# Gated mix of two attentions on one core: one 64-row by 32-column tiling in the steps, relu banks from the scores' ring, output projection in pieces

## Chip, core and metric

The kernel runs on one core of a Trainium2 chip. The metric is the time of one execution on the device in microseconds (us); less is better. Before the change two runs took 2734.1 and 2738.14 us, median 2736.12.

## The reference, cut to what matters

Two attentions over the same input are mixed by a gate. S = 2048, D = 576, 32 heads of 18, all fp32.

```python
def _A_ref(x, wqkv, wo):                       # every head has keys and values of its own
    q, k, v = heads(x @ wqkv)
    p = softmax(einsum("bhqd,bhkd->bhqk", q, k) * 18 ** -0.5)
    return merge(einsum("bhqk,bhkd->bhqd", p, v)) @ wo
def _B_ref(x, wq, wk, wv, wo):                 # 32 query heads share one key and one value head
    ...
x = A_x
g = _sigmoid((x * gate_w).sum(-1, keepdims=True))
return g * a + (1 - g) * b
```

## The kernel before

The 64 heads (`NU`) are numbered u: the 32 of B first, then the 32 of A. A head's scores are 2048 by 2048 and are made transposed, keys on partitions: a *step* is one key tile i of 128 keys of one head, so there are 16 steps per head and `NSTEP` = 1024 in all, counted by T. The loop over T does two steps per pass, A (T) and B (T + 1); one pass is called a turn, eight turns make a head.

**Operands.** A query or key row is kept as high and low fp16 parts: 18 rows high, 18 high or low, 18 low or high, 54 partitions in all, and two more rows for the row maximum, 56 (`load_rows`, `max_rows`). Each operand lies twice in its tile: from partition 0 (`SB`) and from partition 64 (`MB`). A matmul on the first copy uses the upper half of the 128x128 array's rows, one on the second copy the lower half.

**Scores** (`step_scores`, matmul L446, exponential L453). Four matmuls per step, c = 0 to 3, each 128 keys by 512 queries, on the upper half, into a bank of the PSUM pool `ps_s` (3 banks); ScalarE takes the exponential out of the bank into an SBUF tile `pt` (ring of 12).

**Row maxima** (`step_max`, matmul L409) run `LEAD` = 22 steps ahead of the scores, since the scores' 55th and 56th rows subtract the maximum. They are made with queries on partitions: 128 queries by 512 keys on the lower half, into a bank of `ps_m` (4 banks), and VectorE reduces each bank to one column (L418). Of the eight chunks per turn one, A's chunk 1, is replaced by "x": keys of chunk 1 less keys of chunk 0 (`kd`) are multiplied, ScalarE takes the relu (L412) into SBUF, and VectorE adds it in one pass with chunk 0 of the same step (L415), so that VectorE has seven passes per turn and ScalarE nine. In the lead, T < 0, every chunk is reduced, and the maxima alternate with the projection of A's values (`project_v`, L252).

**PV** (`step_pv`, L459). The values with a column of ones, 19 columns, are the stationary operand; the four query chunks j go to four 32-column groups, 128 rows each, all into one bank `acc` that is kept over a head's 16 steps. The operands are fp32. The order strings cut a step's PV into column halves: `p` and `f` are the first and second 256 columns of the step two back, `h` and `H` of the step one back; `P` and `Q` do all 512 at once.

**End of a head** (`head_out`, L469). VectorE copies `acc` to SBUF, from where DMAs place the rows in a tile of 128 output features (`OT`) and the sums in DRAM. `normalise`, a generator advanced one yield per turn, divides the finished features by the sums, times the gate, and splits them on GpSimd into two f32r parts which go to DRAM (`on_d`).

**Output projection** (`out_proj`, matmul L575, evicted at L581 or L583). Three segments: feature tiles 0 to 3, 4 to 7 and 8. A unit is one output tile of 128 rows and 288 columns; it has three products of the split operands over the segment's tiles, 12 matmuls of 128x128 by 288, into a bank of `ps_m`. Segment 0 has its 32 units at fixed steps from T = 522 to 848 (`at_ends`, three in every two heads), segment 1 from 942 to 1008, about one per turn, segment 2 from 1021 on and behind the loop. What is left is the last head (`last_out`).

**Order.** All engines work through their queues in program order. Inside a turn that order is written out by hand as a string: `s` is a score chunk, `m` a maximum chunk, `x` the relu chunk, capitals A and B the step, then the letters of PV, `U` an output unit.

```python
PLAIN = "sA0 mA2 sA1 mA0 sA2 mA3 P sA3 mB0 sB0 mB1 sB1 mB2 h sB2 mB3 sB3 x H"
```

`END` and `AFTER` are used in the two turns around a head's end, `UNIT` where an output unit is due, `ALONE` when no maxima are left.

Of the kernel before, what the change touches and what calls it, by code (L numbers as in the profile page):

```python
# [8 lines left out]
F32 = mybir.dt.float32  # L9
# [5 lines left out]
OP = mybir.AluOpType  # L15
# [34 lines left out]
def gated_mix_kernel(ctx: ExitStack, tc: tile.TileContext, xT, wall, wv, wo, out):  # L50
# [10 lines left out]
    ps_m = ctx.enter_context(tc.tile_pool(name="ps_m", bufs=4, space=PSUM))  # L61
# [13 lines left out]
    on_d = [dram.tile([9 * P, S], F32, name=f"on{x}") for x in "hl"]  # L75
# [10 lines left out]
    acc = ps_o.tile([P, 512], F32, name="acc")  # L86

    nc.vector.memset(acc, 0.0)
# [308 lines left out]
    def step_max(u, i, c, low=False):  # L397
# [10 lines left out]
        pm = ps_m.tile([P, 512], F32, name="pm")  # L408
        nc.tensor.matmul(pm, qs[u % 3][b:b + 54, i * P:(i + 1) * P], k, start=True, stop=True)  # L409
# [30 lines left out]
    def step_scores(u, i, c, alone):  # L440
# [3 lines left out]
        if alone and c % 2:  # L444
            b = MB
        nc.tensor.matmul(ps, kst(u)[b:b + 56, i * P:(i + 1) * P],  # L446
                         qs[u % 3][b:b + 56, c * 512:(c + 1) * 512], start=True, stop=True)
# [8 lines left out]
    def step_pv(u, i, a, b):  # L456

        for j in range(4):
            nc.tensor.matmul(acc[32 * j:32 * j + 19, a:b], v_of(u, i), PT[u, i, j][:, a:b],  # L459
                             start=(i == 0 and a == 0), stop=(i == 15), skip_group_check=True)  # L460
        if b == 512:
            for j in range(4):
                del PT[u, i, j]
# [3 lines left out]
    def head_out(u):  # L467
        oe = L["work"].tile([P, 512], F32, name="oe", bufs=1)
        nc.vector.tensor_copy(oe, acc)  # L469
# [15 lines left out]
    def normalise(t, at_end=False):  # L485
# [32 lines left out]
        for c in range(4):  # L518
            cs = slice(512 * c, 512 * c + 512)
            h = L["work"].tile([P, 512], F32R, name="oh", bufs=1)  # L520
            l = L["work"].tile([P, 512], F32R, name="ol", bufs=1)
            nc.gpsimd.tensor_tensor(ot[:rows, cs], ot[:rows, cs], R[:rows, cs], op=OP.mult)
            yield
            split(ot[:rows, cs], h[:rows], l[:rows], nc.gpsimd, nc.gpsimd)
            yield
            yield
            dma(on_d[0][P * t:P * t + rows, cs], h[:rows])
            dma(on_d[1][P * t:P * t + rows, cs], l[:rows])
# [3 lines left out]

    def prep_wo(t0, rows):
        nt = len(rows)
        w = {y: L["pool"].tile([P, nt, D], F32R, name=f"wo{y}", tag=f"wo{y}{nt}") for y in "hl"}
# [9 lines left out]
    def out_proj(t0, rows, first=False):  # L545

        nt = len(rows)
        oacc = L["oacc"]
        O = {}

        def load(q):
            for x, y in enumerate("hl"):
                if "end" in L:
                    O[q, y] = L["end"][y][:, 256 * q:256 * q + 256].rearrange("p (t s) -> p t s", t=1)
                    continue
                t = L["pool"].tile([P, nt, 256], F32R, name=f"oi{y}", bufs=2)
                dma(t, on_d[x][P * t0:P * (t0 + nt), 256 * q:256 * q + 256]
                    .rearrange("(t p) s -> p t s", p=P))
                O[q, y] = t
# [3 lines left out]
        w = WO[t0]  # L563
        for q in range(8):
            if q < 7:
                load(q + 1)
            o = {y: O[q, y] for y in "hl"}
            for s2 in range(2):
                st_ = 2 * q + s2
                for hf in range(2):  # L570
                    fp = ps_m.tile([P, 512], F32, name="pm")
                    n = 0
                    for a, b in PRODS:
                        for t, r in enumerate(rows):
                            nc.tensor.matmul(fp[:, 0:288], o[b][:r, t, s2 * P:(s2 + 1) * P],  # L575
                                             w[a][:r, t, 288 * hf:288 * hf + 288],
                                             start=(n == 0), stop=(n == 3 * nt - 1))
                            n += 1
# [98 lines left out]
    def due(T, t0, t1, n):  # L677
        if t0 == SEG[0][3]:
            return at_ends.count(T)
# [96 lines left out]
```

## Time and profile before

| | |
|---|---|
| runs, median (lowest to highest) | 2736.12 us (2734.1 to 2738.14) |
| the profiled execution | 2735.79 us; span 2734.0 us |
| granted TensorE clock, mean | 0.991 |
| PE (matmuls), records | 2663.3 us busy, 97%, 22160 |
| VectorE (DVE) | 2430.7 us busy, 89% |
| ScalarE (ACT) | 2384.1 us busy, 87% |
| GpSimd (POOL) | 231.0 us busy, 8% |

PE is TensorE's matmuls and PEld its weight loads; a matmul's record reaches to its modelled end, so records of matmuls that follow each other overlap and a busy PE need not be one at its peak. A row of a timeline has start, length, engine, line, operation, operands and a count (merged records of one kind); a row by line has count, busy us, mean ns of one, and idle time before it with what ended it; a row by source has count, shortest, median and longest ns, and the first and last start. Releasers are inferred from semaphores. The main loop, T >= 0, starts 316 us into the span; the lead lies before it.

### The profile page before, as it was taken

What the parts mean: (1) busy time and instruction counts of PE and PEld (TensorE: products, weight loads), DVE (VectorE), ACT (ScalarE), POOL (GpSimd) and SP (SyncE); (2) the same over time, 40 slices, a digit from 0 to 9 for tenths busy, and PEclk for the clock granted to TensorE, in tenths of its full rate; (3) what the DMA queues carried; (4) which work ended last, traced back from release to release, by engine and by line L of the source; (5) the groups of instructions that cost most, each with busy time, mean ns of one, the idle gap of its engine ahead of it and who ended that gap; (6) DMA issues with size and microseconds to landing.
All of it is one profiled execution on the core that took longest, in us unless ns stands there. A gap on an engine that the chain in (4) does not pass through costs nothing.

```text
span 2734.0 us, 57725 instructions
## 1 busy us (share of the span) xinstructions
PE 2663.3 (97%) x22160; PEld 958.8 (35%) x22160; DVE 2430.7 (89%) x4582; ACT 2384.1 (87%) x4768; POOL 231.0 (8%) x438
## 2 busy tenths in 40 slices
PE   5899999999999999999999999999999999999999
PEld 3688522222222222222222333333333332223444
DVE  5345899999999999999999999999999999998875
ACT  3232499999999999999999999999999999998875
POOL 2221000001000200110110001000100020001000
PEclk9899999999999999999999999999999999999998
DMA  7232100001100100110132112112221122122312
GB/s 197 76 118 90 51 20 20 20 18 53 35 17 23 54 27 20 45 43 20 30 66 85 40 51 84 54 40 57 72 66 47 44 61 64 39 64 88 89 36 94
DMA packets 135321, 151.49 MB, mean 55 GB/s; under 512 B 55709, under 2 KB 104765, under 8 KB 133846
## 3 DMA queue, kind: packets, MB, share of 16 engines
q1 hardware_dynamic: 116156, 123.59, 16.2%
q10 hardware_dynamic: 14120, 13.65, 1.5%
q0 software_dynamic: 4768, 10.56, 1.2%
q8 instruction: 174, 2.85, 0.5%
q14 instruction: 103, 0.84, 0.1%
HBM read 92.02 MB, written 46.45 MB: 51 GB/s over the span
## 4 chain that ended last, share of the span: by engine, by line
ACT 54%; PE 37%; DVE 6%; DMA 2%; SPq 1%; issue 1%; DVEq 0%; ACTq 0%
ACT pt L453 48%; PE acc L459 12%; PE ps L446 11%; ACT xb L412 6%; PE ps L210 6%; PE pm L575 4%; DVE mx L418 3%; PE ps L252 2%; PE pm L409 2%; SPq L56 1%; DVE oe L469 1%; DVE junk L415 1%; DMA xs<-xT 0%; DVE oacc L629 0%; DVE oacc L583 0%
## 5 line engine op out<-in xcount | busy, mean ns | idle before, releaser
L453 ACT ACTIVATE pt<-ps 128x512 f32<-128x512 f32 x4052 | 2093.1, 637 | 68.4 <-PE pm L409 60.2
L418 DVE TENSOR_REDUCE mx<-pm 128x1 f32<-128x512 f32 x3096 | 1940.2, 682 | 89.5 <-PE pm L409 74.6
L446 PE MATMUL ps<-qs,ksb 56*128 56x512 f16 x2688 | 818.4, 380 | 10.8
L409 PE MATMUL pm<-ksb,qs 54*128 54x512 f16 x2364 | 738.5, 383 | 2.6 <-DVE mx L418 1.6
L459 PE MATMUL acc<-pt,vb 128*19 128x512 f32 (+1 forms) x6136 | 592.3, 458 | 1.9
L459 PE MATMUL acc<-pt,vg 128*19 128x256 f32 (+1 forms) x5664 | 579.5, 481 | 2.3 <-DVE oe L469 0.5
L409 PEld LDWEIGHTS <-qs 54*128 54x128 f16 x4096 | 330.0, 93 | 248.1 <-issue 195.2
L446 PE MATMUL ps<-qs,ksa 56*128 56x512 f16 x1364 | 404.4, 379 | 4.8 <-ACT pt L453 1.3
L446 PEld LDWEIGHTS <-ksb 56*128 56x128 f16 x2688 | 175.0, 94 | 622.5 <-issue 573.9
L409 PE MATMUL pm<-ksa,qs 54*128 54x512 f16 x1232 | 384.8, 382 | 0.6 <-ACT xb L412 0.4
L415 DVE CUSTOM_DVE_ANT_0 junk<-pm,xb 128x512 bf16<-128x512 f32 x500 | 339.9, 680 | 0.0
L412 ACT ACTIVATE xb<-pm 128x512 f32<-128x512 f32 x500 | 316.5, 633 | 0.0
L446 PEld LDWEIGHTS <-ksa 56*128 56x128 f16 x1408 | 89.3, 94 | 328.9 <-issue 299.0
L459 PEld LDWEIGHTS acc<-pt,vb 128*19 128x19 f32 x6136 | 104.1, 96 | 223.7 <-issue 206.6
L459 PEld LDWEIGHTS acc<-pt,vg 128*19 128x19 f32 x5664 | 96.0, 97 | 222.9 <-issue 204.9
L428 POOL TENSOR_SCALAR mt<-mt 128x32 f32<-128x32 f32 x64 | 18.6, 290 | 1616.4 <-DVE mt L426 1616.4
L214 ACT ACTIVATE ph<-ps,tv 128x512 f16<-128x512 f32 x56 | 38.5, 687 | 122.0 <-PE ps L210 114.5
L409 PE MATMUL pm<-kdb,qs 54*128 54x512 f16 x372 | 141.5, 380 | 0.0
L220 DVE SCALAR_TENSOR_TENSOR pl<-ps,tv,ph 128x512 f16<-128x512 f32 x56 | 42.0, 751 | 93.8 <-ACT ph L214 75.4
L210 PE MATMUL ps<-xh,wh 128*128 128x512 f32 x280 | 76.4, 403 | 3.3 <-DVE xh L277 2.6
L210 PE MATMUL ps<-xh,wl 128*128 128x512 f32 x280 | 75.1, 399 | 0.0
L469 DVE COPY oe<-acc 128x512 f32<-128x512 f32 x63 | 43.6, 692 | 30.0 <-PE acc L459 29.4
(123 smaller groups left out, 1253.8 us busy)
## 6 DMA issues: line engine op xcount, KB each, us to landing
qs<-qkh SPq DMA_DIRECT2D x244, 72.0 KB
qs<-qkl SPq DMA_DIRECT2D x122, 72.0 KB
onh<-oh SPq DMA_DIRECT2D x32, 256.0 KB
onl<-ol SPq DMA_DIRECT2D x32, 256.0 KB
oih<-onh SPq DMA_DIRECT2D x16, 512.0 KB
oil<-onl SPq DMA_DIRECT2D x16, 512.0 KB
ot<-oe SPq DMA_DIRECT2D x220, 36.0 KB
R<-r_d SPq DMA_DIRECT2D x55, 144.0 KB
```

Of the source, the lines that this page charges most:

```text
L210: nc.tensor.matmul(fp, w[a][:kr, k, :], X[b][:kr, k, cs], start=(n == 0), stop=(n == len(PROJ) - 1))
L220: nc.vector.scalar_tensor_tensor(l, fp, t, h, op0=OP.mult, op1=OP.subtract)
L252: nc.tensor.matmul(fp[:, 0:288], X[b][:kr, k, st_ * P:(st_ + 1) * P], w[a][:kr, k, :], start=(n == 0), stop=(n == len(PROJ) - 1))
L409: nc.tensor.matmul(pm, qs[u % 3][b:b + 54, i * P:(i + 1) * P], k, start=True, stop=True)
L412: nc.scalar.activation(MX["x", u, i], pm, AF.Relu)
L415: nc.vector.tensor_tensor_reduce(junk, pm, MX.pop(("x", u, i)), 1.0, -3e38, op0=OP.add, op1=OP.max, accum_out=MX[u][:, i, c:c + 1])
L418: nc.vector.tensor_reduce(MX[u][:, i, c:c + 1], pm, axis=AX.X, op=OP.max)
L446: nc.tensor.matmul(ps, kst(u)[b:b + 56, i * P:(i + 1) * P], qs[u % 3][b:b + 56, c * 512:(c + 1) * 512], start=True, stop=True)
L453: nc.scalar.activation(pt, ps, AF.Exp, scale=SCALE / LIFT ** 2)
L459: nc.tensor.matmul(acc[32 * j:32 * j + 19, a:b], v_of(u, i), PT[u, i, j][:, a:b], start=(i == 0 and a == 0), stop=(i == 15), skip_group_ch ...
L469: nc.vector.tensor_copy(oe, acc)
L575: nc.tensor.matmul(fp[:, 0:288], o[b][:r, t, s2 * P:(s2 + 1) * P], w[a][:r, t, 288 * hf:288 * hf + 288], start=(n == 0), stop=(n == 3 * nt ...
```

## The change

All matmuls of the main loop's turns use tiles of 64 rows and 32 columns.

- A score or maximum chunk is four matmuls of 32 stationary columns (`quarters`) in place of one of 128.
- PV is split by rows as well: rows 0 to 63 accumulate in `acc[0]`, rows 64 to 127 in `acc[1]`, eight matmuls in place of four. At a head's end VectorE copies one bank, ScalarE the other, and GpSimd adds them.
- PSUM: `ps_s` keeps 3 banks and now also holds the relu chunk; `ps_m` has 2 in place of 4; `acc` has 2 in place of 1; one bank, `ps_u`, is for output units in the loop and, in the lead, for every third maximum.
- The output projection multiplies in fp32 without splitting, so one product in place of three; `normalise` writes one array in place of two and GpSimd's splits go. It has segments of 3, 2, 2 and 1 feature tiles from T = 400, 622, 826 and 938, and the ninth as before. A unit is cut into pieces of one tile, 144 columns and one row half, four matmuls each (`halves`); `lo` pieces first, `hi` pieces when at least three maxima have been issued since. Each `y` in an order string issues one piece, `E` evicts a finished unit, now always on VectorE. Units left at T = 1004 are done whole.
- The order strings are new: `BASE` for plain turns and head ends alike, and one string by unit size.

```diff
-    ps_m = ctx.enter_context(tc.tile_pool(name="ps_m", bufs=4, space=PSUM))
+    ps_m = ctx.enter_context(tc.tile_pool(name="ps_m", bufs=2, space=PSUM))
+    ps_u = ctx.enter_context(tc.tile_pool(name="ps_u", bufs=1, space=PSUM))
...
+    acc = [ps_o.tile([P, 512], F32, name=f"acc{h}") for h in range(2)]
...
+    def quarters(o, w, x, start=True, stop=True):
+        for j in range(0, P, 32):
+            nc.tensor.matmul(o[j:j + 32, :], w[:, j:j + 32], x, start=start, stop=stop, skip_group_check=True)
+
+    def halves(o, prods, cuts):
+        out = []
+        for b in (0, 64):
+            todo = [(w, x, c) for w, x in prods if w.shape[0] > b for c in cuts]
+            out.append([lambda w=w, x=x, c=c, n=n, b=b, m=len(todo):
+                        quarters(o()[:, c], w[b:b + 64], x[b:b + 64, c], b + n == 0, b == 64 and n >= m - len(cuts))
+                        for n, (w, x, c) in enumerate(todo)])
+        return out
...
-        pm = ps_m.tile([P, 512], F32, name="pm")
-        nc.tensor.matmul(pm, qs[u % 3][b:b + 54, i * P:(i + 1) * P], k, start=True, stop=True)
+        L["n"] = (L.get("n", 0) + 1) % 3
+        if c == "x":
+            pm = ps_s.tile([P, 512], F32, name="ps")
+        elif "pt" not in L and L["n"] == 0:
+            pm = ps_u.tile([P, 512], F32, name="pu")
+        else:
+            pm = ps_m.tile([P, 512], F32, name="pm")
+        quarters(pm, qs[u % 3][b:b + 54, i * P:(i + 1) * P], k)
...
-        nc.tensor.matmul(ps, kst(u)[b:b + 56, i * P:(i + 1) * P],
-                         qs[u % 3][b:b + 56, c * 512:(c + 1) * 512], start=True, stop=True)
+        quarters(ps, kst(u)[b:b + 56, i * P:(i + 1) * P], qs[u % 3][b:b + 56, c * 512:(c + 1) * 512])
...
-        for j in range(4):
-            nc.tensor.matmul(acc[32 * j:32 * j + 19, a:b], v_of(u, i), PT[u, i, j][:, a:b],
-                             start=(i == 0 and a == 0), stop=(i == 15), skip_group_check=True)
+        for h in range(2):
+            r = slice(64 * h, 64 * h + 64)
+            for j in range(4):
+                nc.tensor.matmul(acc[h][32 * j:32 * j + 19, a:b], v_of(u, i)[r], PT[u, i, j][r, a:b],
+                                 start=(i == 0 and a == 0), stop=(i == 15), skip_group_check=True)
...
-        nc.vector.tensor_copy(oe, acc)
+        nc.vector.tensor_copy(oe, acc[0])
+        nc.scalar.activation(oe1, acc[1], AF.Copy)
+        nc.gpsimd.tensor_tensor(oe, oe, oe1, op=OP.add)
...
-            split(ot[:rows, cs], h[:rows], l[:rows], nc.gpsimd, nc.gpsimd)
...
-            dma(on_d[0][P * t:P * t + rows, cs], h[:rows])
-            dma(on_d[1][P * t:P * t + rows, cs], l[:rows])
+            dma(on_d[P * t:P * t + rows, cs], ot[:rows, cs])
...
+                lo, hi = halves(bank, [(O[q][:, t, s0:s0 + P], w[:, t, 288 * hf:288 * hf + 288])
+                                       for t in range(nt)], (slice(0, 144), slice(144, 288)))
...
+    def piece():
+        if unit() and (now["T"] < 994 or len(cur["lo"]) < 2):
+            if cur["lo"]:
+                cur["lo"].pop(0)()
+                cur["m"] = 0
+            elif cur["hi"] and cur["m"] >= 3:
+                cur["hi"].pop(0)()
...
+    for t0, nt, T in ((0, 3, 400), (3, 2, 622), (5, 2, 826), (7, 1, 938)):
+        when(T - 20, lambda t0=t0, nt=nt: load_wo(t0, nt))
+        when(T, lambda t0=t0, nt=nt: side.append(out_units(t0, nt)))
...
+    when(1004, lambda: todo.append(whole_units()))
+    when(1017, lambda: todo.append(last_proj(8, rows)))
...
+    BASE = "sA0 mB1 sA1 p sA2 mA0 f mB3 sA3 sB0 mA2 x sB1 mA3 h mB0 sB2 H sB3 mB2"
+    SIDE = {
+        3: "sA0 mB0 sA1 E p sA2 mA0 f mB3 sA3 y x sB0 mA2 h mA3 sB1 y sB2 mB1 H sB3 mB2 y",
+        2: "y mB3 sA0 p mA3 sA1 f mB1 sA2 y sA3 mA0 y x y y y y y y sB0 E mB0 h mB2 sB1 H sB2 mA2 sB3",
+        1: "E mB0 p sA0 mB3 f sA1 mA3 y x y sA2 mA0 h mB1 y sA3 y sB0 mB2 H mA2 sB1 y sB2 y sB3 y y y",
+    }
...
+        order = LEADS if T < 0 else FIRST if T == 0 else ALONE if alone else \
+            SIDE[cur["size"]] if unit() and (T < 994 or len(cur["lo"]) < 2) else BASE
```

147 lines of the change are left out of this document (85 added, 62 removed).

## Prediction

> **What bounds the kernel now.** I read the page's busy times and chain first, then the rate of the main loop by stages (the relu at L412 runs once per turn, a turn being one pass of the step loop, two key tiles), then the timeline inside a turn.
>
> ```profile
> PE 2663.3 (97%) x22160; PEld 958.8 (35%) x22160; DVE 2430.7 (89%) x4582; ACT 2384.1 (87%) x4768; POOL 231.0 (8%) x438
> ACT 54%; PE 37%; DVE 6%; DMA 2%; SPq 1%; issue 1%; DVEq 0%; ACTq 0%
> ```
>
> Three engines are near full. The chain lies mostly on ACT, and what is not ACT's is nearly all PE's. The rates, from the first and last start and the count of the relu rows in four windows:
>
> ```profile
> L412 ACT ACTIVATE xb<-pm x254: 608/641/717, 342.1 to 1476.6; 128x512 f32<-128x512 f32 x127
> ...
> L412 ACT ACTIVATE xb<-pm x164: 603/612/642, 1483.4 to 2257.6; 128x512 f32<-128x512 f32 x164
> ...
> L412 ACT ACTIVATE xb<-pm x49: 603/641/718, 2262.3 to 2479.7; 128x512 f32<-128x512 f32 x49
> ...
> L412 ACT ACTIVATE xb<-pm x30: 603/603/641, 2479.7 to 2647.2; 128x512 f32<-128x512 f32 x30
> ```
>
> That is 4.48 us per turn without output units (1134.5/253), 4.75 with the first segment's units (774.2/163), 4.53 after them (217.4/48), and 5.78 (167.5/29) where the second segment puts a unit in every turn. The floors of the two evicting engines come from runs of equal instructions and from the mean durations:
>
> ```profile
> 2641.47 0.39 PE L446 MATMUL ps<-qs,ksa 56*128 56x512 f16 x1
> 2641.47 0.39 PE L409 MATMUL pm<-ksa,qs 54*128 54x512 f16 x1
> 2641.89 1.57 ACT L453 ACTIVATE pt<-ps 128x512 f32<-128x512 f32 x3
> 2641.92 0.69 DVE L418 TENSOR_REDUCE mx<-pm 128x1 f32<-128x512 f32 x1 [0.82 <-PE pm L409]
> ...
> 2643.14 2.48 DVE L418 TENSOR_REDUCE mx<-pm 128x1 f32<-128x512 f32 x4
> ```
> ```profile
> L453 ACT ACTIVATE pt<-ps 128x512 f32<-128x512 f32 x4052 | 2093.1, 637 | 68.4 <-PE pm L409 60.2
> L418 DVE TENSOR_REDUCE mx<-pm 128x1 f32<-128x512 f32 x3096 | 1940.2, 682 | 89.5 <-PE pm L409 74.6
> ```
>
> Four reductions in 2.48 with 0.68 each are 0.60 apart, and three exponentials in 1.57 with 0.64 each 0.47 to 0.48. A turn has 8 exponentials and a relu, 9 x 0.48 = 4.3 us of ACT, and 7 reductions, 4.2 of DVE. So a plain turn of 4.48 stands 0.18 above ACT's floor: whatever happens to PE, little can be won there. The expensive places are the turns with output units. The same rows give the handoffs: from a matmul's start to its reduction 0.45, to its exponential 0.42 to 0.43.
>
> **The change part by part.** First, what it takes from PE:
>
> ```profile
> 1001.37 0.63 PE L459 MATMUL acc<-pt,vb 128*19 128x256 f32 x8
> 1001.93 0.39 PE L446 MATMUL ps<-qs,ksb 56*128 56x512 f16 x1
> ...
> 1002.15 0.38 PE L446 MATMUL ps<-qs,ksb 56*128 56x512 f16 x1
> ...
> 1002.41 0.39 PE L409 MATMUL pm<-ksb,qs 54*128 54x512 f16 x1
> 1002.72 1.06 PE L459 MATMUL acc<-pt,vb 128*19 128x512 f32 x8
> 1003.71 0.39 PE L446 MATMUL ps<-qs,ksb 56*128 56x512 f16 x1
> ```
>
> A score matmul lasts 0.22 (1001.93 to 1002.15). A PV block of 512 columns holds PE 0.99, one of 256 columns 0.56: 256 columns cost 0.43 (two passes, so x8 for four matmuls), and 0.13 is spent leaving the column tiling; entering costs 0.31 - 0.22 = 0.09. Three blocks a turn make 0.66 us of drains, which go. With 64x32 tiles each row half has per turn 8 x 0.22 for its scores or maxima and four PV blocks of 0.45: 3.56 us. PE stops being the fullest engine.
>
> Second, what takes the drains' place. The maxima had four banks with the relu; they now have two, and seven reductions a turn. The scores' ring of three takes the relu too, 9 users for 8. When a bank comes free I read here:
>
> ```profile
> 1014.89 1.11 ACT L453 ACTIVATE pt<-ps 128x512 f32<-128x512 f32 x2
> ...
> 1016.05 0.37 PE L446 MATMUL ps<-qs,ksb 56*128 56x512 f16 x1
> ```
>
> ACT ends at 1016.00 and the waiting matmul starts 0.05 later; I take the same for DVE. Four quarters start one after another, which I cost below at 0.02 for the fourth. One round of a maximum's bank is 0.45 + 0.02 + 0.68 + 0.05 = 1.20, so two banks can just feed a reduction every 0.60, DVE's own pace: no slack is left, and every moment for which PE isn't ready at the release is lost. One round of a score's bank is 0.43 + 0.02 + 0.64 + 0.05 = 1.14. Following BASE entry by entry in program order, the loop that closes is: mB0, its bank's round to the next turn's mB1 (1.20), sA1's matmul (0.22), the block p before sA2 (0.45), mA0's matmul on the other half (0.22), block f (0.45), then sA3, its bank's round to sB1 (1.14), mA3 (0.22), block h (0.45) back to mB0; four times an entry is queued behind eight instructions of the one before (0.03 each). Sum 1.20 + 1.14 + 0.66 + 1.35 + 0.12 = 4.47. What waits behind those entries on PE's one queue is everything else: behind mB1 stand sA1 and p, behind sB1 stand mA3 and h, and ACT waits for them. Per head DVE has two things more:
>
> ```profile
> L469 DVE COPY oe<-acc 128x512 f32<-128x512 f32 x63 | 43.6, 692 | 30.0 <-PE acc L459 29.4 <-DMA oih<-onh 0.5
> ```
> ```profile
> 296.95 1.28 DVE L418 TENSOR_REDUCE mx<-pm 128x1 f32<-128x512 f32 x2
> ...
> 298.26 0.22 DVE L424 TENSOR_REDUCE m<-mx 128x16 f32<-128x64 f32 x1
> ...
> 298.65 1.25 DVE L418 TENSOR_REDUCE mx<-pm 128x1 f32<-128x512 f32 x2
> ```
>
> The copy takes 0.6 of its time (the next block p waits for it and for ACT's copy of the other half), the row maxima 0.5 (a reduction would have followed at 296.95 + 1.20 = 298.15). In its turn each goes beyond the 0.27 that DVE has free, and block p comes later; I add 0.45 for each, 0.9 per head or 0.11 per turn (bounds 0 and 1.4 per head). A plain turn becomes 4.58, against 4.48.
>
> Third, the instructions. A turn had 16 + 24 matmul records and as many weight loads, 80; it gets 64 + 64 of each, 256. How fast they can be supplied the trace bounds from two sides:
>
> ```profile
> 1016.44 0.14 PEld L459 LDWEIGHTS acc<-pt,vb 128*19 128x19 f32 x8 [0.29 <-issue]
> ...
> 36.35 0.41 PE L239 MATMUL pm<-ident,pst 18*128 18x18 f32 x4
> ...
> L239 PE MATMUL pm<-ident,pst 18*128 18x18 f32 x16 | 1.7, 215 | 0.0
> ```
>
> Eight loads of 0.10 in 0.14, with four matmuls between, are 3 to 4 ns per instruction, in a burst that had been queued. Four tiny transposes in 0.41 with 0.215 each are 65 ns per pair, 30 ns per instruction. I take 4 ns, since the burst also goes to different column tiles, as the quarters do; the other end gives a rival.
>
> Fourth, the output units. They took 1.8 us of PE each:
>
> ```profile
> 2643.96 0.80 PE L575 MATMUL pm<-woh,oih 128*128 128x288 f32 x4
> ...
> 2645.76 0.39 PE L446 MATMUL ps<-qs,ksa 56*128 56x512 f16 x1
> ...
> L583 DVE TENSOR_TENSOR oacc<-pm,oacc 128x288 f32<-128x288 f32 x64 | 27.4, 455 | 23.5 <-PE pm L575 23.5
> ```
>
> Now they are pieces of 144 columns in fp32, 144/256 x 0.43 + 0.02 = 0.26 us on one row half, in a bank that no other work waits for. By the conditions in `piece` a unit of three tiles takes 4 turns, of two tiles 2 turns, of one tile 1 turn. Each half has 4.47 - 3.56 = 0.9 free per turn, but not in one stretch: I add 0.1 per turn to the three pieces of size 3 (bounds 0 and 0.78), 0.25 to the four of size 2 that run in a row (0 and 1.04), and for size 1, where DVE evicts a unit (0.46) every turn, 0.15. Turns: 4.68, 4.83, 4.73. The splits that leave POOL, the fewer transfers on SP's queue and POOL's added sum cost nothing: POOL is at 8%, and heads are 36 us apart; without that cover the sum's transfer would be late by under a microsecond per head.
>
> Fifth, the lead before the first scores:
>
> ```profile
> 238.00:315.00 77.00, 77.00 (x536) 62.99 (x534) 53.28 (x88) 13.78 (x34) 2.24 (x12) 1.00 0.23 76
> ...
> 297.92 0.73 PE L409 MATMUL pm<-ksb,qs 54*128 54x512 f16 x4
> ```
>
> PE is full there, and the 88 maxima come in 22 groups of four, whose last starts 0.36 after the first. With three banks (`ps_m` and `ps_u` in rotation) the fourth waits for the first's round, 1.20; about 0.85 later, 22 x 0.85 = 19 us, with the value projection queued behind it. At the end the output rings shrink from four banks to two; round times against 0.40 per eviction give some 8 us (0 to 15).
>
> **The sum**, by steps T: 0 to 406, 203 turns x 0.10 = +20; 406 to 526, 60 x (4.68 - 4.48) = +12; 526 to 662, 68 x (4.68 - 4.75) = -5; 662 to 796, 67 x (4.83 - 4.75) = +5; 796 to 857, 30 turns, -2; 857 to 942, 43 x (4.83 - 4.53) = +13; 942 to 1002, 30 x 5.78 = 173 becomes 9 x 4.83 + 17 x 4.73 + 4 x 4.58 = 142, -31. Together +12, with lead and end +39. The profiled execution took 2735.8 (span 2734.0 and 1.8 around it), as the runs' median 2736.1: 2775 us, 1.4% more. About 2% is what a measurement here tells from no change.
>
> **Rivals.** (a) PE's instruction supply decides. For it speaks that no row sustains more; against it, the burst. It decides outright from 4.47/256 = 17 ns; at 30 ns a turn is 7.7 and the time 2736 + 512 x 3.2 = 4370. At 10 ns the four queue steps grow from 0.03 to 0.08: +0.2 per turn, some 2880. The Trainium skill (TensorE: Matmul & The Clock Gate, "Wait — 56ns, not 53.3ns?") gives about 25 ns as the least between matmul starts; were that a floor for each of the 256 instructions, an estimate by it is 6.4 us per turn and some 3720. The burst's loads start closer than that, on different column tiles. (b) The other side: row halves run ahead of each other so that no entry waits behind a PV block, and a bank's round stays under 1.20. Then the evictors decide: plain turn 4.38, with pieces 4.45 to 4.7; 203 x -0.10, 128 x -0.2, 140 x -0.2, -36 for the last 30, +27: about 2655. For it speaks the 0.9 us free on each half; against it, two banks without slack. (c) Weight loads are exposed. The Trainium skill (TensorE: Matmul & The Clock Gate, "Part 3: Packing small matmuls — row/col tiling", "The mechanism") has loads overlap running matmuls only on another row group. By rows:
>
> ```profile
> 1019.99 0.39 PE L446 MATMUL ps<-qs,ksb 56*128 56x512 f16 x1
> ...
> 1020.00 0.10 PEld L446 LDWEIGHTS <-ksb 56*128 56x128 f16 x1
> ...
> 1020.21 0.38 PE L446 MATMUL ps<-qs,ksb 56*128 56x512 f16 x1
> ```
>
> here a load starts 0.01 after a matmul of its own half and the next follows at 0.22, so the trace contradicts. If it held in the new tiles, 12 loads x 0.095 per half and turn, +1.1: 3300. (d) The tiling doesn't hold: halves or quarters don't run side by side, or switches stay. Half rate for f16 quarters makes 8 x 0.44 + 1.8 = 5.3 per turn: 3170.
>
> **Chances.** Forecast 0.55 (its own range 2710 to 2830), (a) 0.20, (b) 0.15, (c) 0.05, (d) 0.05. Of the forecast 0.40 lies within 2% (up to 2791), 0.15 above; of (a) 0.02 within; of (b) 0.13 below 2681, 0.02 within. Faster 0.13, same 0.44, slower 0.43. The range 2690 to 2900 reaches into (b) and through the mild end of (a).
>
> **What would show it.** Right: relu rows 4.5 to 4.6 apart in plain turns, near 4.8 with size 2; PE waiting at L409's line on DVE and L446's on ACT; ACT under 90%; a lead some 19 us longer. Wrong: instruction starts evenly spaced with PE waiting for nothing (a), plain turns below 4.45 (b), same-half matmuls 0.3 apart (c) or 0.44 apart (d).

## The result, and the profile after

The changed kernel takes 2825.1 us (median of two runs, 2823.6 to 2826.6), the kernel before 2736.1: a ratio of 1.0325, 95% interval 1.0281 to 1.037. It is 89 us slower, where the forecast was 39. The profiled execution took 2823.6 us, its span is 2821.8; what follows is in its numbers. First the busy times of the page:

```profile
PE 2672.4 (95%) x74588; PEld 1709.5 (61%) x74588; DVE 2517.1 (89%) x4680; ACT 2434.3 (86%) x4799; POOL 234.5 (8%) x421
```

PE, DVE and ACT are as busy as before, at more than three times the matmuls. These totals hide where the time went. The rate by stages shows it; the relu (now L436, still one per turn) gives it with the first and last start and the count, in stretches with one kind of turn each:

```profile
L436 ACT ACTIVATE xb<-ps x197: 597/604/608, 343.2 to 1247.0; 128x512 f32<-128x512 f32 x197
...
L436 ACT ACTIVATE xb<-ps x198: 597/604/608, 363.0 to 1270.3; 128x512 f32<-128x512 f32 x198
L436 ACT ACTIVATE xb<-ps x58: 589/592/594, 1292.5 to 1559.4; 128x512 f32<-128x512 f32 x58
...
L436 ACT ACTIVATE xb<-ps x65: 592/603/608, 1902.2 to 2209.2; 128x512 f32<-128x512 f32 x65
L436 ACT ACTIVATE xb<-ps x42: 597/603/606, 2341.2 to 2539.4; 128x512 f32<-128x512 f32 x42
L436 ACT ACTIVATE xb<-ps x27: 591/603/642, 2553.6 to 2678.1; 128x512 f32<-128x512 f32 x27
...
L436 ACT ACTIVATE xb<-ps x10: 591/618/642, 2644.1 to 2689.0; 128x512 f32<-128x512 f32 x10
```

A turn takes 4.61 us without units (907.3/197; forecast 4.58), 4.68 with units of three tiles (266.9/57; forecast 4.68), 4.80 and 4.83 with two (307.0/64 and 198.2/41; forecast 4.83), 4.79 with one (124.5/26; forecast 4.73). The first relu starts at 343.2 instead of 321.6, and the last at 2689.0 instead of 2647.2. The kernel before in the same view, in two windows:

```profile
L412 ACT ACTIVATE xb<-pm x207: 597/641/717, 321.6 to 1249.4; 128x512 f32<-128x512 f32 x104
...
L412 ACT ACTIVATE xb<-pm x2: 603/603/603, 2641.3 to 2647.2; 128x512 f32<-128x512 f32 x2
```

From the last relu on, the old kernel needs 86.9 us to the end of its span (2734.0 - 2647.2), the new one 132.8 (2821.8 - 2689.0). This table sets the prediction's terms beside the differences of the two profiled executions, each read from the relu's starts at those steps:

| stretch (steps T) | predicted us | before | after | difference |
|---|---|---|---|---|
| lead, to the first relu | +19 | 321.6 | 343.2 | +21.6 |
| 0 to 406 | +20 | 907.6 | 929.4 | +21.8 |
| 406 to 526 | +12 | 271.0 | 280.6 | +9.6 |
| 526 to 662 | -5 | 323.0 | 324.0 | +1.0 |
| 662 to 796 | +5 | 317.3 | 321.3 | +4.0 |
| 796 to 857 | -2 | 147.6 | 146.2 | -1.4 |
| 857 to 942 | +13 | 189.1 | 202.6 | +13.5 |
| 942 to 1002 | -31 | 163.0 | 135.4 | -27.6 |
| end, from the last relu | +8 | 86.9 | 132.8 | +45.9 |

(The main rows begin at T = 2, the last of them ends at T = 998.) One row is far off: the end. The waits of PE in the whole execution of the changed kernel point there too (us in total, times, the longest):

```profile
PE pu L617 <- DVE oacc L611: 25.9, 6, 24.9
PE pm L96 <- DVE mx L442: 25.2, 75, 0.6
PE acc L484 <- DVE oe L494: 8.5, 45, 0.6
PE pu L96 <- issue: 5.9, 4, 4.2
```

The first row is six waits of which one alone is 24.9 us. The timeline around it, DVE first, then PE, then ACT:

```profile
2714.62 0.46 DVE L611 TENSOR_TENSOR oacc<-pu,oacc 128x288 f32<-128x288 f32 x1 [1.00 <-PE pu L617]
2715.47 0.69 DVE L494 COPY oe<-acc 128x512 f32<-128x512 f32 x1 [0.40 <-PE acc L484]
2724.66 0.95 DVE L524 RECIPROCAL sm<-sm 96x128 f32<-96x128 f32 x1 [8.50 <-DMA sm<-sum_d]
2725.64 0.29 DVE L525 TENSOR_TENSOR sm<-sm,gt 96x128 f32<-96x128 f32 x1
2735.95 0.69 DVE L542 TENSOR_TENSOR ot<-ot,R 110x512 f32<-110x512 f32 x1 [10.01 <-DMA R<-r_d]
...
2743.11 0.45 DVE L611 TENSOR_TENSOR oacc<-pu,oacc 128x288 f32<-128x288 f32 x1
...
2717.63 0.75 PE L617 MATMUL pu<-wo,oi 128*128 128x288 f32 x2
2718.31 0.41 PE L96 MATMUL ps<-qs,ksa 56*32 56x512 f16 x8
2743.61 1.33 PE L617 MATMUL pu<-wo,oi 128*128 128x288 f32 x2 [24.89 <-DVE oacc L611]
...
2745.60 1.09 ACT L476 ACTIVATE pt<-pm 128x512 f32<-128x512 f32 x2 [25.69 <-PE pm L96]
```

PE writes an output unit at 2717.63. Its eviction, a sum of 0.45 us on DVE, runs at 2743.11. DVE rests for most of the time in between: the last normalisation stands ahead of it in DVE's one queue and waits 8.50 us for a transfer of the sums, then 10.01 for the spread reciprocals, and then does its twelve operations (7.2 us). The next unit wants the same single bank, so PE waits, with all scores queued behind, and ACT waits 25.69 us. The kernel before has the same two transfers at its end (its DVE, then a wait of its PE from 2647 us on):

```profile
2679.87 0.95 DVE L497 RECIPROCAL sm<-sm 96x128 f32<-96x128 f32 x1 [6.78 <-DMA sm<-sum_d]
...
2691.52 0.69 DVE L515 TENSOR_TENSOR ot<-ot,R 110x512 f32<-110x512 f32 x1 [10.38 <-DMA R<-r_d]
...
2698.69 1.67 DVE L583 TENSOR_TENSOR oacc<-pm,oacc 128x288 f32<-128x288 f32 x4
```
```profile
PE pm L575 <- DVE oacc L583: 0.2, 1, 0.2
```

There four evictions stand behind them at 2698.69, but the units have four banks, and PE waits 0.2 us for an eviction.

### The profile page after: what moved, and what is told of

Same layout as the page of the kernel before. It is cut to its first block, busy times and chain, and to the rows that moved or that the text cites. A ratio compares the mean times of both kernels' runs of the same rounds, so it can differ in the third digit from the quotient of the medians.

```text
span 2821.8 us, 167296 instructions
## 1 busy us (share of the span) xinstructions
PE 2672.4 (95%) x74588; PEld 1709.5 (61%) x74588; DVE 2517.1 (89%) x4680; ACT 2434.3 (86%) x4799; POOL 234.5 (8%) x421
## 3 DMA queue, kind: packets, MB, share of 16 engines
q8 instruction: 583, 9.55, 1.5%
## 5 line engine op out<-in xcount | busy, mean ns | idle before, releaser
L442 DVE TENSOR_REDUCE mx<-pm 128x1 f32<-128x512 f32 x3067 | 1944.4, 684 | 46.8 <-PE pm L96 23.1
L96 PEld LDWEIGHTS <-qs 54*32 54x32 f16 x16384 | 662.3, 89 | 548.3 <-issue 325.2
L96 PE MATMUL ps<-qs,ksb 56*32 56x512 f16 x10752 | 971.9, 381 | 0.6 <-ACT pt L476 0.4
L96 PE MATMUL pm<-ksb,qs 54*32 54x512 f16 x9340 | 931.3, 381 | 35.6 <-DVE mx L442 20.2
L484 PE MATMUL acc<-pt,vg 64*19 64x256 f32 x16384 | 715.4, 377 | 5.5 <-DVE oe L494 3.0
L484 PE MATMUL acc<-pt,vb 64*19 64x256 f32 x16384 | 688.0, 376 | 6.7 <-DVE oe L494 5.5
L96 PE MATMUL pm<-ksa,qs 54*32 54x512 f16 x4928 | 504.5, 381 | 7.5 <-DVE mx L442 4.7
L96 PE MATMUL ps<-qs,ksa 56*32 56x512 f16 x5456 | 498.1, 381 | 1.5 <-ACT pt L476 0.6
L96 PEld LDWEIGHTS <-ksb 56*32 56x32 f16 x10752 | 361.0, 89 | 180.5 <-issue 97.8
L96 PE MATMUL pu<-wo,oi 64*32 64x144 f32 x7616 | 398.8, 283 | 5.9 <-issue 5.9
L439 DVE CUSTOM_DVE_ANT_0 junk<-pm,xb 128x512 bf16<-128x512 f32 x500 | 344.6, 689 | 27.6 <-issue 4.7
L484 PEld LDWEIGHTS acc<-pt,vg 64*19 64x19 f32 x16384 | 323.9, 95 | 70.2 <-DVE oe L494 14.1
L436 ACT ACTIVATE xb<-ps 128x512 f32<-128x512 f32 x500 | 300.6, 601 | 2.3 <-PE ps L96 2.1
```

The costliest lines, as they stand in the source:

```text
L96: nc.tensor.matmul(o[j:j + 32, :], w[:, j:j + 32], x, start=start, stop=stop, skip_group_check=True)
L436: nc.scalar.activation(MX["x", u, i], pm, AF.Relu)
L439: nc.vector.tensor_tensor_reduce(junk, pm, MX.pop(("x", u, i)), 1.0, -3e38, op0=OP.add, op1=OP.max, accum_out=MX[u][:, i, c:c + 1])
L442: nc.vector.tensor_reduce(MX[u][:, i, c:c + 1], pm, axis=AX.X, op=OP.max)
L484: nc.tensor.matmul(acc[h][32 * j:32 * j + 19, a:b], v_of(u, i)[r], PT[u, i, j][r, a:b], start=(i == 0 and a == 0), stop=(i == 15), skip_gr ...
```

## The experiments

Times are those of one execution unless an interval is given. The kernel before ran beside them on their chip: 2731.8 us beside the first four, 2735.1 beside the second four, 2734.3 beside the rest.

**e1_spread: the last normalisation in steps.** Instead of all at once at T = 1010, its generator is advanced a few parts at a time, so that evictions come between its waits.

```
+                yield
...
-    when(16 * (NU - 1) + 2, lambda: run(normalise(8, at_end=True)))
+    ends = {}
...
+    for T_, n_ in ((1010, 2), (1012, 1), (1014, 2), (1016, 1), (1018, 1), (1020, 1), (1022, 2)):
+        when(T_, lambda n_=n_: end_step(n_))
```

> The changed kernel, except that the division of the last feature tile (normalise of tile 8) is no longer emitted at once at T = 1010 but a step at a time in the turns from 1010 to 1022, so that VectorE's evictions of whole output units do not stand in its queue behind two DMA round trips. Theory (the queue behind a DMA wait cost the end): the 24.9 us in which PE waited for the eviction at L611 go, total 2797 to 2803 us against 2823.6. Rival (the end is slow because whole fp32 units, switches of tiling and the rings of two banks are slow): PE's long wait may go but the time comes back elsewhere, total within 5 us of 2823.6.

Measured: 2805.1 us, 2 above the range of the theory and far from the rival. The longest of PE's waits from 2690 us on is now

```profile
PE pu L618 <- DVE oacc L612: 3.6, 6, 2.5
```

and the stretch after the last relu falls from 132.8 to 111.7 us: the queue behind the normalisation was worth 21 us. About 25 us of the longer end remained.

**e5_ring: three banks at the end.** On top of e1_spread, the last projection and the last head's output take the units' bank as a third one in rotation.

```
+    def end_bank():
+        L["eb"] = (L.get("eb", 0) + 1) % 3
+        if L["eb"] == 2:
+            return ps_u.tile([P, 512], F32, name="pu")
+        return ps_m.tile([P, 512], F32, name="pm")
...
-                fp = ps_m.tile([P, 512], F32, name="pm")
+                fp = end_bank()
...
-                ps = ps_m.tile([P, 512], F32, name="pm")
+                ps = end_bank()
```

> e1_spread (the last normalisation taken in steps) and, at the end, three banks in rotation in place of two for the last projection and the last head's output (the output's own bank, idle by then, is the third). My theory: with two banks an eviction of 0.51 us comes every 0.60 instead of every 0.43 in the kernel before; a third bank gives that back: 32 x 0.17 = 5.5 us, and some 3 for the last projection's units behind the last scores: 9 us less than e1_spread, near 2796. The rival, that the extra at the end is PE's own work (fp32 units and the merging of the two sums): 0 to 2 us less than e1_spread.

Measured: 2797.1, 8.0 less. The evictions of the last head's output, first in e1_spread, then in e5_ring (counts, durations, first and last start):

```profile
L667 DVE SCALAR_TENSOR_TENSOR oacc<-pm,rl,oacc x32: 517/518/519, 2780.1 to 2798.6; 128x288 f32<-128x288 f32 x32
```
```profile
L673 DVE SCALAR_TENSOR_TENSOR oacc<-pm,rl,oacc x22: 506/506/506, 2778.2 to 2791.3; 128x288 f32<-128x288 f32 x22
L673 DVE SCALAR_TENSOR_TENSOR oacc<-pu,rl,oacc x10: 506/506/506, 2779.0 to 2790.5; 128x288 f32<-128x288 f32 x10
```

32 evictions come 18.5/31 = 0.60 us apart with two banks and 13.1/31 = 0.42 with three, which is the pace of the kernel before (0.43). The stretch after the last relu falls from 111.7 to 100.5 us, by 11.2; the whole falls by 8.0 only, since the last relu starts 3.9 us later in this run (2694.8 against 2690.9) though nothing is changed before it. These are the rings that the prediction priced at 8 us (0 to 15), and 11 lies within.

**e4_lead: four banks in the lead.** Every fourth maximum before the first scores takes a bank of the scores' ring.

```
-        L["n"] = (L.get("n", 0) + 1) % 3
-        if c == "x":
+        L["n"] = (L.get("n", 0) + 1) % 4
+        if c == "x" or "pt" not in L and L["n"] == 2:
```

> The changed kernel, except that in the lead the maxima rotate over four banks (one of them from the scores' ring) in place of three. Theory (the fourth maximum of each group of four waits for the first one's bank, 0.85 to 1 us in 22 groups): the first relu comes at 322 to 326 us in place of 343, total 18 to 21 us less. Rival (the lead is longer because of the four times as many instructions or the new switches of tiling): the first relu stays at 343.

Measured: 2806.5. The first relu starts at 323.8 us, where the kernel before has 321.6:

```profile
L436 ACT ACTIVATE xb<-ps x201: 597/603/608, 323.8 to 1246.0; 128x512 f32<-128x512 f32 x101
```

So 19.4 of the 21.6 us of the longer lead are the missing fourth bank. The 2.2 left are within what runs with one and the same lead differ by (first relu at 339.6 to 344.4 us in six runs with three banks there).

**e3_order, e2_third, e7_third: the plain turn.** e3_order moves entries of the order only:

```
-    BASE = "sA0 mB1 sA1 p sA2 mA0 f mB3 sA3 sB0 mA2 x sB1 mA3 h mB0 sB2 H sB3 mB2"
+    BASE = "sA0 sA1 mB1 p sA2 mA0 f sA3 mA3 x sB0 mA2 h sB1 mB3 sB2 mB0 H sB3 mB2"
```

> The changed kernel with one string changed: the plain turn's order becomes sA0 sA1 mB1 p sA2 mA0 f sA3 mA3 x sB0 mA2 h sB1 mB3 sB2 mB0 H sB3 mB2. The same entries, instructions, banks and evictions per turn. Theory (the plain turn is a loop of two bank rounds and three PV blocks that one entry after the other waits for in PE's queue): with this order that loop is cut, the evicting engines decide, and the plain turn falls from 4.60 to about 4.48 us (8 turns 35.9 in place of 36.7), total some 25 us less. Rival (instruction supply, or anything that only counts instructions): no change, within 4 us.

e2_third leaves the order and gives the maxima a third bank (the units' own, where no unit is under way), though at uneven distances because its count also runs on the relu; e7_third counts the maxima alone.

```
-        elif "pt" not in L and L["n"] == 0:
+        elif L["n"] == 0 and ("pt" not in L or not side and not cur):
...
-        L["n"] = (L.get("n", 0) + 1) % 3
+        L["n"] = (L.get("n", 0) + (c != "x")) % 3
```

(the last two lines in e7_third alone)

> The changed kernel, except that in turns where no output unit is pending every third maximum uses the bank ps_u, so the maxima have three banks there in place of two (T = 0 to 400 and some 18 turns later). Theory (the round of a maximum's bank sits in the loop that sets the plain turn): relu rows of T = 2 to 406 fall from 4.60 us per turn to 4.44 to 4.50, total 20 to 33 us less. Rival (instruction supply, 256 instructions per turn, sets 4.47): the plain turn stays at 4.60 and the total within 4 us of 2823.6.

> The changed kernel with a third bank for the maxima wherever no output unit is under way (in e2_third the count of the rotation also ran on the relu's chunk, so the third bank came at uneven distances; here it takes every third maximum). If two banks without slack set the plain turn, 4.41 to 4.45 with this order and 203 + some 60 turns gain 0.12 each: 2823.6 - 30 = 2794. If the order is what binds, with the scores' ring shared between eight scores and the relu behind PV blocks in one queue (my reading after e2_third and e3_order): plain turns stay at 4.46 to 4.48, and only the turn at the head's end gains, as in e2_third: 2815 to 2822.

Measured: e3_order 2804.6, e2_third 2819.7, e7_third 2803.6. The relu in the first stretch, in the order e3_order, e2_third, e7_third:

```profile
L436 ACT ACTIVATE xb<-ps x196: 588/592/650, 363.7 to 1246.3; 128x512 f32<-128x512 f32 x196
```
```profile
L436 ACT ACTIVATE xb<-ps x194: 602/607/672, 362.0 to 1245.4; 128x512 f32<-128x512 f32 x194
```
```profile
L436 ACT ACTIVATE xb<-ps x196: 597/603/677, 363.8 to 1246.2; 128x512 f32<-128x512 f32 x196
```

That is 4.53, 4.58 and 4.53 us per turn, against 4.61 in the changed kernel. The same mean comes about in two ways. Of the eight turns of a head the changed kernel has six at 4.46 to 4.48, and two longer ones, 5.00 where the sums are copied out and 4.89 where DVE makes the row maxima. With the new order the six fall to 4.41 to 4.47, and the second long turn to 4.49 to 4.54. With the even third bank the six stay at 4.46, the second long turn goes and the first falls to 4.83. e3_order gave 19 us where some 25 were expected. Neither expectation for e7_third held as a whole: the plain turn did what the second said, but the third bank is worth 15 us in this stretch, all of it in the turns in which DVE does something else; the 4.46 of the plain turn is the order's, not the bank count's alone. e2_third missed its theory. By the total, 4.0 us less, it looks like the rival there, instruction supply; but e3_order has as many instructions and takes 19 us less, so that the rival does not hold. That the uneven rotation spoiled e2_third fits e7_third, which differs in nothing else.

**b1_quarters and b2_banks: one part of the change alone, on the kernel before.** b1_quarters writes scores and maxima in quarters; b2_banks has the change's banks.

```
+    def quarters(o, w, x):
+        for j in range(0, P, 32):
+            nc.tensor.matmul(o[j:j + 32, :], w[:, j:j + 32], x, start=True, stop=True, skip_group_check=True)
...
-        nc.tensor.matmul(pm, qs[u % 3][b:b + 54, i * P:(i + 1) * P], k, start=True, stop=True)
+        quarters(pm, qs[u % 3][b:b + 54, i * P:(i + 1) * P], k)
```
```
-    ps_m = ctx.enter_context(tc.tile_pool(name="ps_m", bufs=4, space=PSUM))
+    ps_m = ctx.enter_context(tc.tile_pool(name="ps_m", bufs=2, space=PSUM))
...
-        pm = ps_m.tile([P, 512], F32, name="pm")
+        pm = ps_s.tile([P, 512], F32, name="ps") if c == "x" else ps_m.tile([P, 512], F32, name="pm")
```

> The kernel before with one thing changed: each score and each maximum is written as four matmuls of 32 columns in place of one of 128 (the PV blocks, the banks and the output projection stay as they were). A plain turn goes from 80 matmuls and weight loads to 176. My theory (an instruction costs PE 3 to 4 ns, and the four quarters run side by side): plain turns stay at 4.45 to 4.55 us, the whole at 2730 to 2765. The rival that instruction supply decides: at 10 ns per instruction the 96 more add 0.96 us of issue to a PE that is 97% busy, +0.7 per turn or more, above 3000; at 25 ns above 3700. If the quarters don't run side by side, 16 x 0.66 more per turn: above 7000.

> The kernel before with the banks of the change and nothing else: two banks for the maxima in place of four, the relu's bank from the ring of the scores (the two banks set free stay unused; matmuls, orders and output projection as before). My theory (two banks with a round of 1.20 us can just feed DVE, and on one undivided PE queue each round also holds a PV block of 0.99 and a drain): plain turns 5.0 to 5.7, the whole 3000 to 3350, PE and DVE waiting for each other at the maxima. The rival, that the bank count is harmless and the orders or the units made the loss: below 2780. The lead is longer too, by 20 to 40 us.

Measured: b1_quarters 2766.5, b2_banks 3433.2. The busy row of b1_quarters, then the waits of b2_banks and its relu:

```profile
PE 2704.0 (98%) x46736; PEld 1029.2 (37%) x46736; DVE 2445.3 (88%) x4582; ACT 2413.2 (87%) x4768; POOL 231.1 (8%) x438
```
```profile
DVE mx L418 <- PE pm L409: 624.2, 1290, 3.5
ACT pt L453 <- PE pm L409: 597.8, 969, 2.0
...
L412 ACT ACTIVATE xb<-ps x192: 605/605/619, 403.6 to 1498.2; 128x512 f32<-128x512 f32 x192
```

b1_quarters has 24,576 more matmuls than the kernel before (46,736 against 22,160) and as many more weight loads, and takes 31.4 us longer: 0.64 ns for each instruction added, on a PE whose records fill 98% of the span. What of an instruction's own time was hidden beside other work is not in that figure. It ended 1.5 us above my range, but at a sixteenth of the milder rival's 10 ns. A steady limit of instruction supply is not what the change lost by. b2_banks was slower than I had expected: 1094.6/191 = 5.73 us per turn where I gave 5.0 to 5.7. In the old tiling and order, two banks for the maxima and the relu in the scores' ring cost 1.24 us per turn. The changed kernel, with the same banks, pays 0.11. So tiling and order together make two banks nearly enough; no run tells which of them does it.

**t1_tiling: the tiling alone.** The kernel before with quarters, PV in row halves and two sums, three banks for the maxima, the relu in the scores' ring, and one order for plain turns; the output projection stays. Of the edit only the orders are shown.

```
+    PLAIN = "mB1 sA0 mA3 x mA2 p sA1 mB0 sA2 f sA3 mB3 sB0 mA0 h sB1 mB2 sB2 H sB3"
+    UNIT = "mB1 x U sA0 mA3 sA1 mA2 p sA2 mB0 f sA3 mB3 sB0 mA0 h sB1 sB2 mB2 H sB3"
```

> The kernel before with the tiling alone: scores and maxima in quarters of 32 columns, PV in row halves with two sums in two banks (one bank is taken from the maxima's four, and the relu's bank is from the scores' ring), one order for plain turns as in e8_open and one for turns with a unit; output projection, its schedule and the end stay as before. My theory (the order holds a plain turn at ACT's pace, 4.41 to 4.44 with 0.2 per head; a unit still takes both halves for 1.8 us and costs about 1.3 per turn, as before): 330 plain turns gain 0.06 each, unit turns 0 to 0.2, the merged sums cost 1: 2736 - 20 to 30 = 2706 to 2716, 0.99 of the kernel before. The rival that 64 x 32 tiles themselves cost (more instructions, half the contraction): not under 2730.

Measured over three rounds: 2750.3, a ratio of 1.0056 to the kernel before, 95% interval 1.004 to 1.0073. The gain that I expected did not come. The relu of its first stretch:

```profile
L423 ACT ACTIVATE xb<-ps x202: 603/763/802, 341.7 to 1249.7; 128x512 f32<-128x512 f32 x101
```

908.0/201 = 4.52 us per turn, no less than the 4.48 that the kernel before has. Its plain turns do take 4.41, but those of the kernel before take 4.41 to 4.54, and the turns at the head's end, 4.77 to 4.86 with two copies and a sum to merge, take the rest: an undisturbed head is 35.8 us in t1_tiling and 35.9 in the kernel before. On top come three turns of 6.8 to 8.3 us (T = 144, 256, 368) in which PE stops for 1.6 to 1.8 us and nothing in the profile releases it; the kernel before has no such stop. From the last relu to the end it takes 100.7 us, against 86.9; 6.8 of that only mean that its relu stands early in the turn, so some 7 us are a longer end. The timelines of a plain turn in e8_open (below) show what holds a turn of 4.41: neither evictor rests. DVE, then ACT:

```profile
1014.52 0.69 DVE L443 TENSOR_REDUCE mx<-pu 128x1 f32<-128x512 f32 x1
1015.27 1.29 DVE L443 TENSOR_REDUCE mx<-pm 128x1 f32<-128x512 f32 x2
1016.47 0.68 DVE L443 TENSOR_REDUCE mx<-pu 128x1 f32<-128x512 f32 x1
1017.07 1.34 DVE L443 TENSOR_REDUCE mx<-pm 128x1 f32<-128x512 f32 x2
1018.32 0.68 DVE L440 CUSTOM_DVE_ANT_0 junk<-pu,xb 128x512 bf16<-128x512 f32 x1
1018.93 0.08 DVE L440 DVE_READ_ACCUMULATOR2_ANT mx<- 128x1 f32 x1
...
1016.24 0.76 ACT L437 ACTIVATE xb<-ps 128x512 f32<-128x512 f32 x1
1016.78 4.14 ACT L477 ACTIVATE pt<-ps 128x512 f32<-128x512 f32 x8
1020.65 0.76 ACT L437 ACTIVATE xb<-ps 128x512 f32<-128x512 f32 x1
```

From 1014.52 to 1018.93 on DVE, and from 1016.24 to 1020.65 on ACT, nothing rests for more than 0.06 us, and both stretches are 4.41 us. No kernel here keeps up a faster pace over a head, but that 4.41 is the least is not shown: after a delay single turns come at 4.30 (e8_open, t1_tiling), and ACT's relu takes 0.76 us in the turn shown, against 0.60 in the changed kernel.

**e6_all and e8_open: the repairs together.** e6_all is e5_ring with the lead's four banks and the order of e3_order. e8_open adds, in turns without units, the even third bank and the order that t1_tiling has.

```
...
+    OPEN = "mB1 sA0 mA3 x mA2 p sA1 mB0 sA2 f sA3 mB3 sB0 mA0 h sB1 mB2 sB2 H sB3"
...
-            SIDE[cur["size"]] if unit() and (T < 994 or len(cur["lo"]) < 2) else BASE
+            SIDE[cur["size"]] if unit() and (T < 994 or len(cur["lo"]) < 2) else BASE if side else OPEN
```

> The changed kernel with the four repairs together: the last normalisation in steps, three banks at the end, four banks for the maxima of the lead (every fourth from the scores' ring), and the plain turn's order of e3_order. Apart they gave 18.5, an expected 9, 17 and 19 us; if they add, 2823.6 - 63 = 2760 (2755 to 2768): still 25 us above the kernel before, which is what the turns with pieces and the turns of the end would then hold. If they hide one another, above 2775.

> e6_all with, in the turns without output units, three banks for the maxima in even rotation and another order (two maxima ahead of each exponential's score, the relu early): mB1 sA0 mA3 x mA2 p sA1 mB0 sA2 f sA3 mB3 sB0 mA0 h sB1 mB2 sB2 H sB3. A recurrence over the banks with the durations of the trace gives a round of eight turns 35.3 (ACT's pace of 4.41 per turn) against 36.0: about 0.09 x 220 turns = 20 us less than e6_all: 2735. If something besides banks and order holds a plain turn at 4.47, no less than 2750.

Measured: e6_all 2755.1, so the four repairs add (68 us together, 63 expected). e8_open 2745.3, half of the 20 us more that I expected: its plain turns are at 4.41, but the first turn of each head stays at 4.86. That is 11 us above the kernel before, and no version came below the kernel before.

**e9_nounits: without the units of the end.** e6_all, with the 18 units left out that fall into the turns without maxima.

```
                 if unit():
-                cur["whole"]()
                 cur.clear()
                 yield
```

> e6_all without the 18 fp32 output units that it still has to do after the last maxima, three per turn (their matmuls and evictions are left out, so 18 of the 32 tiles of the seventh block's product are missing from the output; all else stays). What is left of the longer end in e6_all is 103.3 us from the last relu against 86.9 in the kernel before. My theory: those units hold both halves of PE for 0.70 us each in turns in which PE is the fullest engine, 18 x 0.70 = 12.6 us: the end falls to 89 to 92 us, the whole to 2741 to 2744. The rival, that the two sums and their merging or the order of the turns without maxima hold the end: the units would lie beside ACT's work, and the end stays above 97, the whole above 2749.

Measured: 2745.8; from the last relu to the end 98.9 us instead of 103.3. The end is where the rival put it (above 97), the whole lies between the two theories. Of the 9.4 us by which the span is shorter, only 4.4 lie in the end; 5.0 lie before the last relu, where the two kernels have the same instructions (this run lacks a stop of PE that the other has, see below). The trace shows how the 4.4 come about. The six turns from T = 1004 on took 35.2 us with the units and take 24.2 without (three of them 5.3, four now 3.8): the 11 us that my theory expected. But now the last projection comes before its input, and PE and ACT wait:

```profile
PE pm L585 <- DVE endh L141: 9.2, 1, 9.2
...
2689.28 0.69 DVE L542 TENSOR_TENSOR ot<-ot,R 110x512 f32<-110x512 f32 x1 [11.04 <-DMA R<-r_d]
...
2692.72 1.09 ACT L476 ACTIVATE pt<-ps 128x512 f32<-128x512 f32 x2 [10.65 <-PE ps L96]
```

The turn at T = 1016 grows from 7.8 to 17.0 us: the same transfers, no longer hidden, take 9 of the 11 us back, and 2.6 are gained behind the last turn's start. The units were cover for the transfers.

## Why the prediction was right or wrong

**The step that failed is the end, "+8 (0 to 15)".** It measured +45.9. What it named, the output rings, gave 11 us of that stretch when a third bank was added, within its range. Two things were put at nothing, and no reason was given. First, the eviction of a unit stands behind the last normalisation in DVE's queue: e1_spread took 21 us away by moving nothing else. The prediction had listed what a new wait holds up for the main loop, but not for the end, where the change puts units, evicted by DVE through one bank, behind an old DMA wait that had cost nothing. Second, 18 of the 32 units of one tile do not run in the turns up to T = 1002, whose saving the prediction booked in full at -31 (measured -27.6), but in the turns after; its own sum has only 17 turns for 32 such units and no price for those left over. Six turns that take 25.6 us in the kernel before take 37.4 in e5_ring with these units. The 21 and the 11 of the rings are 32 of the 46, shown by repairs. Their extra 12 us would fill most of the 14 that are left, and e9_nounits takes 11 out of these turns; but its end became shorter by 4.4 only, and t1_tiling, which has none of these units, has an end some 7 us longer too. So what holds the last 14 us is argued, not shown.

**The plain turn was right in size, and only partly for the reason given.** 4.61 was measured against 4.58, the head's extra 0.94 per head (36.70 for eight turns, less 8 x 4.47) against 0.9. The loop of 4.47 goes through a maximum's bank and a score's bank. PE's waits show the first (25.2 us on L442); on ACT's release of a score's bank it waited 1.0 us in three places. e3_order shows that the order holds the six plain turns, e7_third that a third bank alone doesn't free them, although it opens the loop as I drew it at the maximum's bank. So that the size came out at 4.47 is in part luck. That the score's bank is what closes the loop stays argued.

**The lead was right**: +21.6 against +19, and e4_lead gives 19.4 of them back.

**The turns with pieces were right** within 0.06 us per turn. The term for T 526 to 662 missed by 6 us, and one turn explains it: at T = 590 a turn takes 11.3 us in the changed kernel and 10.4 to 11.7 in the eight versions e1 to e8. In it PE stops between the first and the second quarter of one piece, where nothing in the code waits:

```profile
1708.98 0.11 PEld L96 LDWEIGHTS pu<-wo,oi 64*32 64x32 f32 x1
...
1713.61 0.19 PEld L96 LDWEIGHTS pu<-wo,oi 64*32 64x32 f32 x6 [4.53 <-issue]
```

Behind the stop the granted clock is 0.69 (1709 to 1716 us) and 0.80 (1716 to 1722). e9_nounits has the instructions of e6_all up to there, and takes 5.2 us for that turn.

**Rival (a), instruction supply, fell as a steady limit**: in b1_quarters an added instruction cost 0.64 ns, e3_order won 19 us with as many instructions, and the tiled kernels issue 256 per 4.41 us. But the stop above looks like a late fetch of code. The queue that carries instructions moved 9.55 MB instead of 2.85, and its 16 KB transfers start 4.1 us apart (median, 320 to 2640 us). Just ahead of the stop 8.3 us pass between two of them, from 1702.4 to 1710.7; the versions e1 to e8 have a gap of 8.0 to 8.6 us at the same place, and e9_nounits, without the stop, has none there (4.1 us). What made the transfer late is open: all transfers together were at 102 GB/s in the 9 us before the stop, against a mean of 50, but at 104 in e9_nounits too. The Trainium skill's floor of some 25 ns between matmul starts (TensorE: Matmul & The Clock Gate, "Wait — 56ns, not 53.3ns?") does not hold across tiles in this trace: of the changed kernel's matmuls from 400 to 1200 us, 82% start less than 25 ns after the one before. **Rival (b), the evictors' pace of 4.38 per turn, fell for want of anything to win**: the pace reached is 4.41, the order of the change misses it by 0.06, and the kernel before is within 0.13 of it outside the head's end. **(c) and (d) fell**: the f16 quarters of one half follow each other at 0.22 us (scores at 1004.28 and 1004.50 of the changed kernel), and quarters and row halves run side by side (maxima at 1004.31 on the other half).

Of the signs that I named, ACT under 90% was a poor one: it was 87% before and is 86% now.

## What to carry to other kernels

Before a step's eviction is moved to an engine, write down what stands ahead of it in that engine's queue at every place where it can run, the ends of the program too: a wait for a transfer that costs nothing while nobody waits behind it costs up to its full length as soon as a one-bank producer does. Work that is moved out of a full stretch is not saved until the stretch that it moves into is priced, and the work that leaves may have been the cover of a transfer. And an engine at 97% need not be the bound when two others run almost without a gap: read the evictors' pace from their timelines first, and compare it with the turn as it is.

## What the runs showed of the hardware

An added matmul or weight load made the run 0.64 ns longer when four matmuls of 32 columns took the place of one of 128 (b1_quarters, PE's records at 98%). I had taken 4.

PE can stop for some 4 us with nothing to wait for in the code: at T = 590, in nine runs of ten with the pieces, right behind a gap of 8 us between the transfers of the instruction queue.

After the 24.9 us of waiting, PE ran slow for some time. The granted clock (after the busy times, before the DMA share) in four windows of the changed kernel:

```profile
2700.00:2718.00 18.00, 16.72 (x328) 6.96 (x312) 4.81 (x10) 14.39 (x28) 1.27 (x1) 1.00 0.08 19
2718.00:2743.00 25.00, 0.72 (x10) 0.11 (x8) 8.02 (x14) 1.08 (x2) 0.00 (x0) 0.58 0.22 53
2743.00:2748.00 5.00, 4.39 (x44) 1.58 (x52) 1.37 (x4) 1.09 (x2) 0.00 (x0) 0.50 0.00 2
2748.00:2752.00 4.00, 3.79 (x76) 1.67 (x60) 0.57 (x2) 2.76 (x6) 0.00 (x0) 0.84 0.01 4
```

A unit took 1.33 us at 2743.61 and 0.75 at 2717.63. So the price of a long wait is its length and, by an estimate from these windows, up to 3 us more. The Trainium skill has PE return to its full clock after about 3.4 us of sustained work (TensorE: Matmul & The Clock Gate, "Part 1: The HAM clock gate (the "warmup" mystery)"); here work goes on at 2743.61, the clock is at half until 2748 and at 0.84 for the next 4 us, which is 1.3 us more at half: 5.7 us, longer than the Trainium skill has it.
